# Odd token tiles carried to a later pair: layer two of a fused attention and MLP kernel, with another order of loads and an earlier first visit

## The chip, the cores and the metric

The kernel runs on one core of a Trainium2 chip. The metric is the device time of one execution in microseconds (us); less is better. TensorE is PE in the profile, VectorE DVE, ScalarE ACT, GpSimd POOL, SyncE SP.

## The reference

```python
def _attn_ref(q, k, v):                       # q, k, v: (8, 12, 448, 64), float32
    scores = q @ k.T / sqrt(64) - log(448)    # per batch and head
    attn = 1 / (1 + exp(-scores))             # sigmoid, no softmax
    return attn @ v
def _moe_ref(x, w_in, w_out, beta):           # x: (3584, 768); d_ff = 2048
    h = x @ w_in
    g = h * (1 / (1 + exp(-beta * h)))        # beta: one number per column of h
    return g @ w_out                          # (3584, 768), float32
# x is the attention output, heads side by side: 8 batches x 448 tokens, 12 x 64 columns
```

## The kernel before

Everything is computed in fp16 with fp32 sums in PSUM; the loads cast on the way. The 24 groups of four heads of a batch are called quads, three to a batch (QPB = 3).

**Attention in visits.** A visit computes the scores of one quad against 128 keys (jt = 0, 1, 2), or of one or two quads against the last 64 keys (jt = 3), into four PSUM banks, and one sigmoid on ACT (`weigh_two`, L257; `weigh`, L242 where it fills two banks) writes the weights to slots of the tile `attns`, which has 14 of them (NAT). From quad 3 on the visits stand in the list `visits`, numbered 0 to 73. `attend` (L332) multiplies a finished quad's weights with v; DVE copies the result to xT. The first batch goes in half visits, written out by hand in `BEGIN`.

**Layer one.** The first two batches are done by plain matmuls (`dense1`, L354), in groups of six, each followed by a sigmoid on ACT (L366) and a product on DVE (L369) that writes the hidden tile `gt`. Batches 2 to 7 go in pairs through `blocks`: a scheme of seven products for two batches at once (L523), 168 matmuls with 16 others between them. `first_layer` runs such a block at the visit that `turns` names. `gt` holds two batches (896 tokens, a window of NTILE = 7 tiles of 128), so each window is overwritten by the next.

**Layer two.** The 28 tiles of tokens are multiplied with w_out in halves of 384 columns. A pair of neighbouring tiles t and t + 1 goes by `strassen` (L643): seven products of eight matmuls, 56 in all. The sums of hidden halves that the products read are made on DVE two products ahead (`hidden_sum`, L630). A plain tile (`dense2`, L384) takes 32. Since a window has seven tiles, one is odd: in window 0 tiles 0, 1, 2 are plain and 3 to 6 two pairs; in windows 1 to 3 there are three pairs and a single tile (13, 20, 27) by `single` (L437), of 32 matmuls. The last tile's products are cut in pieces of 256 and 128 columns (CUTS), which ACT copies out (L399) and `store` writes.

**What sets the order.** The matmuls of layers one (plain) and two stand in a list `fill`. After each visit the loop at the end spends some of them: a pace, so that what is left spreads over the visits up to the next turn, plus a correction per visit from the table MORE (in units of 0.164 us); LATE says after how many matmuls attention values may go. TensorE's order is thus fixed when the kernel is built. `hidden_sum`, copies and transposes go to DVE's queue, loads to POOL's queue in the order of the lists LOADS and LATER and then of the visits, at most eight in flight; stores go to SP's queue.

Of the kernel before, what the change touches and what calls it, by code (L numbers as in the profile page):

```python
# [13 lines left out]
def kernel(  # L14
# [84 lines left out]
    NAT = 14  # L99
# [275 lines left out]
    def release(key):  # L375
        touch(held.pop(key))
        m2s.pop(key)
# [16 lines left out]
    def leave(t: int, half: int, m2, piece=None):  # L394
        lo, hi = half * HALF, (half + 1) * HALF
        if piece is not None:
            release((t, half, piece))
            lo, hi = CUTS[piece : piece + 2]
            nc.scalar.copy(out=osbs[t][:, lo:hi], in_=m2)  # L399
            store(t, lo, hi)  # L400
            return
# [5 lines left out]
        if t == NT - 1:  # L407
            store(t, lo, hi)
        elif left[t] == 2:
            store(t, 0, DM)  # L410

    CUTS = (0, 2 * P, HALF)

    def sum_of_halves(t: int):
        sums[t, 0] = sump.tile([P, ND, P], FP16, tag="sum", name="sum")
        nc.vector.tensor_tensor(out=sums[t, 0], in0=hid(t, 0), in1=hid(t, 1), op=ALU.add)

    def single(t: int, n: int, dc: int, piece=None):

        if (n, dc) == (0, 0):  # L420
            if (t, 0) not in sums:
                sum_of_halves(t)
            for half in range(1 + (t < NT - 1)):
                m2s[t, 1 - half] = bank(HALF, (t, 1 - half))
        if piece is not None and (n, dc) == (1, 0):
            m2s[t, 0, piece] = bank(CUTS[piece + 1] - CUTS[piece], (t, 0, piece))
        both = sums[t, 0]
        half, x, w = (
            (1, hid(t, 0), B12),
            (0, hid(t, 1), B21),  # L430
            (1, both, B22),
            (0, both, B11),
        )[n]
        m2 = m2s[(t, half) if piece is None else (t, half, piece)]
        stop = n > 1 and dc == ND - 1
        w = w[:, dc] if piece is None else w[:, dc, CUTS[piece] : CUTS[piece + 1]]
        nc.tensor.matmul(m2, x[:, dc], w, start=(n < 2 and dc == 0), stop=stop)  # L437
        if stop:
            leave(t, half, m2, piece)

    NT = NTOK // P

    def cols(t: int):
        return slice(t % NTILE * P, (t % NTILE + 1) * P)

# [186 lines left out]
    def strassen(t: int, i: int, dc: int):  # L632

        name, x, _, op, w = product(t, i)
        if dc == (ND // 2 if i == 0 and t % NTILE == 0 else 0) and i + 2 < NPROD:
            hidden_sum(t, i + 2)
        if (t, i, dc) == (NT - 3, NPROD - 2, 0):
            sum_of_halves(NT - 1)
        first = (t, name) not in m2s
        if first:  # L640
            m2s[t, name] = bank(HALF, (t, name))
        m2 = m2s[t, name]
        nc.tensor.matmul(  # L643
            m2,
            (x if op is None else sums[t, i])[:, dc],
            w[:, dc],
            start=first,
            stop=(dc == ND - 1),
            skip_group_check=i >= 4,
        )  # L650
        if dc < ND - 1:
            return
        if i == 0:
            for u in (t, t + 1):
                osbs[u] = outp.tile([P, DM], FP32, tag="osb", name="osb")
        L, R = slice(0, HALF), slice(HALF, DM)
        o1, o2 = osbs[t], osbs[t + 1]
        r, a = m2s.get((t, "r")), m2s.get((t, "a"))

        def add(out, in0, in1, op=ALU.add):  # L660
            nc.vector.tensor_tensor(out=out, in0=in0, in1=in1, op=op)  # L661

        if i == 1:
            nc.scalar.copy(out=o2[:, L], in_=a)  # L664
        elif i == 2:
            nc.vector.tensor_copy(out=o1[:, L], in_=m2)
            add(o1[:, R], r, o1[:, L])
            release((t, "s"))
        elif i == 3:
            add(o2[:, L], m2, o2[:, L])  # L670
            release((t, "b"))
        elif i == 4:
            add(o2[:, R], a, o2[:, L], ALU.subtract)
# [11 lines left out]
    def store(t: int, lo: int, hi: int):  # L685
        osb = osbs[t]
        c, end = t * P, (t + 1) * P
        while c < end:
            b, i = divmod(c, S)
            rows = out[b * S : (b + 1) * S, lo:hi]  # L690
            if b == B - 1:
                n = min(end - c, S - i, P if t == NT - 1 else ROWS)
# [9 lines left out]
    def pairs(first: int, n: int):  # L702
        for t in range(first, first + 2 * n, 2):
            for i in range(NPROD):
                for dc in range(ND):
                    opens = i in (2, 3) or (i == 4 and dc < ND // 2)
                    yield M2_US, lambda a=(t, i, dc): strassen(*a), opens

    def alone(t: int):
        order = [(n, None) for n in range(4)]  # L710
        if t == NT - 1:
            order = [(0, None), (2, None), (1, 0), (3, 0), (1, 1), (3, 1)]
        for n, piece in order:
            for dc in range(ND):
                yield M2_US, lambda a=(t, n, dc, piece): single(*a), n < 3
# [27 lines left out]
    def window(w: int):  # L743
        yield from pairs(w * NTILE, 3)
        yield from alone((w + 1) * NTILE - 1)
# [11 lines left out]
    with tc.manual_schedule():  # L757
        def load(what, *a):
# [21 lines left out]
            ("qk", 3), ("w_out", 0, 0), ("w_out", 1, 0), ("values", 1), ("qk", 4), ("qk", 5), ("w_out", 0, 1),  # L780
# [24 lines left out]
        still = const.tile([P, 512], FP16, name="still")  # L805
# [16 lines left out]
        def beta_columns():  # L822
# [14 lines left out]
            ("q", 3, 0), ("q", 3, 1), ("dense", 45),  # L837
# [29 lines left out]
        fill += list(pairs(3, 2))  # L867
# [17 lines left out]
        def left_us(n: int):  # L885
# [4 lines left out]
        MORE = {  # L890
# [3 lines left out]
        }  # L894
        RESERVE = (1.99, 3.28)
        LATE = {
            0: 1, 6: 1, 8: 3, 17: 1, 26: 6, 34: 4, 45: 2, 48: 3, 68: 10, 72: 10,
        }
        turns = {4 * QPB: 1, 6 * QPB: 1}
# [35 lines left out]
        def first_layer(b: int):  # L935
# [5 lines left out]
            fill.extend(window(b // 2))  # L941
            blocks(b, fill_units, 2 if b < B - 2 else 0)

        for n, (g, jt, also) in enumerate(visits):
# [17 lines left out]
            some_sum()  # L962
            for f in soon[:2]:
                f()
# [8 lines left out]
            owed = pace + MORE.get(n, 0) * M2_US  # L973
# [3 lines left out]
            while due or (at_fill[0] < len(fill) and fill[at_fill[0]][0] / 2 < owed):  # L977
                if due and (jt >= 1 or clear()) and spent >= LATE.get(n, 0):
                    values(due.pop())
                elif fill[at_fill[0]][0] / 2 < owed or (due and spent < LATE.get(n, 0)):  # L980
# [4 lines left out]
        assert not sums_todo  # L985
        due.append(NQUAD - 1)
# [32 lines left out]
```

## Time and profile before

| | |
|---|---|
| median of 3 runs | 373.27 us (373.2 to 373.52) |
| profiled execution | span 371.2 us from the first to the last instruction; what lies around it is the 2.1 us up to the median |
| granted TensorE clock | 0.999 |
| TensorE matmul | 365.5 us busy, 98% |
| DVE / ACT / POOL | 254.4 / 259.7 / 80.5 us busy |
| first visit of the list, first matmul | 42.12 us |
| last visit (73), first matmul | 298.07 us |
| last matmul, start | 367.77 us |

A line of a timeline is: start, duration, engine, line, operation, what it writes <- what it reads, shape, number, and in brackets the engine's idle time before it with what ended it. A line of waits is: who waited, for whom, us in total, how often, the longest.

### The profile page before, as it was taken

The page shows a single profiled execution, that of the slowest core. Times are in us where ns is not written, and L with a number is a line of the kernel's source. Part 1 is how long each engine was busy: PE and PEld are TensorE (multiplying, and loading weights), DVE is VectorE, ACT ScalarE, POOL GpSimd, SP SyncE. Part 2 cuts the span into 40 slices and gives each one's busy share as a digit, 9 for nine tenths or more (in the row PEclk, how much of TensorE's full clock was granted, in tenths as well). Part 3 has the DMA queues.
Part 4 walks back from the last instruction along what each step waited for, and adds up shares of the span by engine and source line. Part 5 has one row for each costly group of instructions (what it writes and reads, how often), then busy time and mean ns, then how long its engine had stood idle before and what let it go on. Part 6 is the DMA issues. An engine that isn't in the chain of part 4 may idle for free.

```text
span 371.2 us, 7295 instructions
## 1 busy us (share of the span) xinstructions
PE 365.5 (98%) x2906; PEld 184.6 (50%) x2906; DVE 254.4 (69%) x479; ACT 259.7 (70%) x311; POOL 80.5 (22%) x120
## 2 busy tenths in 40 slices
PE   8999999999999999999999999999999999999997
PEld 4566544443444455544444445554444455555665
DVE  4435796777496967787666667778767667679671
ACT  5995766798967668887877749887678647883000
POOL 7732431221131013233131003233100002230000
PEclk9999999999999999999999999999999999999999
DMA  9999999893368030029829410017803111000334
GB/s 173 195 197 204 202 205 206 193 123 51 51 86 174 1 87 1 2 49 130 171 37 212 106 25 20 3 29 110 171 2 85 44 44 42 1 2 1 87 85 129
DMA packets 36226, 34.65 MB, mean 93 GB/s; under 512 B 9424, under 2 KB 32608, under 8 KB 36192
## 3 DMA queue, kind: packets, MB, share of 16 engines
q0 software_dynamic: 30288, 22.47, 42.3%
q1 hardware_dynamic: 5904, 11.71, 11.1%
q8 instruction: 23, 0.38, 0.4%
q14 instruction: 11, 0.09, 0.1%
HBM read 45.62 MB, written 11.01 MB: 153 GB/s over the span
## 4 chain that ended last, share of the span: by engine, by line
PE 93%; ACT 5%; issue 1%; DVE 0%; ACTq 0%
PE ps L643 27%; PE ps L523 26%; PE ps L229 11%; PE ps L332 10%; PE ps L354 9%; PE ps L384 4%; PE ps L437 4%; ACT attns L242 3%; ACT attns L257 1%; PE ps L812 1%; ACT sg L366 1%; DVE gt L369 0%; ACT osb L664 0%; DVE still L806 0%; ACT osb L399 0%
## 5 line engine op out<-in xcount | busy, mean ns | idle before, releaser
L257 ACT ACTIVATE attns<-ps,nlogs 128x1792 f16<-128x1792 f32 x75 | 131.7, 1756 | 41.1 <-PE ps L229 41.0
L643 PEld LDWEIGHTS <-sum 128*128 128x128 f16 x440 | 40.5, 98 | 37.3 <-issue 12.5
L537 POOL TENSOR_TENSOR gt<-attns,sg 128x448 f16<-128x448 f32 x21 | 23.9, 1137 | 141.7 <-ACT sg L534 141.7
L229 PE MATMUL ps<-qT,kT 32*128 32x448 f16 (+3 forms) x864 | 52.3, 339 | 1.1 <-ACT attns L242 0.6
L534 ACT ACTIVATE sg<-ps,beta_sb 128x448 f32<-128x448 f32 x72 | 45.2, 632 | 8.4 <-PE ps L523 5.9
L523 PE MATMUL ps<-xT,w_in 128*128 128x448 f16 x216 | 49.2, 353 | 0.0
L523 PE MATMUL ps<-xT,w_S 128*128 128x448 f16 x216 | 49.2, 352 | 0.0
L643 PE MATMUL ps<-w_T,sum 128*128 128x384 f16 x264 | 48.7, 327 | 0.0
L537 DVE TENSOR_TENSOR gt<-ps,sg 128x448 f16<-128x448 f32 x72 | 44.2, 618 | 4.0 <-ACT sg L534 3.8
L341 DVE CAST xT<-ps 128x448 f16<-128x448 f32 (+1 forms) x54 | 28.8, 567 | 21.5 <-PE ps L332 21.5
L523 PEld LDWEIGHTS <-w_in 128*128 128x128 f16 x288 | 28.0, 98 | 26.6 <-issue 0.7
L661 DVE TENSOR_TENSOR osb<-ps,osb 128x384 f32<-128x384 f32 x55 | 30.5, 554 | 15.1 <-PE ps L643 12.8
L332 PE MATMUL ps<-attns,v 128*64 128x448 f16 (+3 forms) x432 | 40.4, 340 | 0.1
L354 PE MATMUL ps<-xT,w_in 128*128 128x448 f16 (+1 forms) x240 | 39.5, 316 | 0.6 <-DVE gt L369 0.6
L630 DVE TENSOR_TENSOR sum<-gt 128x1024 f16<-128x1024 f16 x55 | 36.5, 678 | 0.2
L369 DVE TENSOR_TENSOR gt<-ps,sg 128x448 f16<-128x448 f32 (+1 forms) x40 | 20.0, 527 | 22.4 <-ACT sg L366 22.3
L125 POOL DMA_DIRECT2D raw<-in_q_dram x26 | 14.4, 555 | 92.8 <-DVE kT L212 84.7
L643 PE MATMUL ps<-w_out,gt 128*128 128x384 f16 x176 | 33.3, 327 | 0.0
L643 PE MATMUL ps<-w_out,sum 128*128 128x384 f16 x176 | 32.3, 327 | 0.0
L583 DVE TENSOR_TENSOR ps<-ps,attns 128x448 f32<-128x448 f32 x24 | 15.2, 632 | 23.3 <-PE ps L523 19.4
L523 PEld LDWEIGHTS <-w_S 128*128 128x128 f16 x216 | 21.1, 98 | 19.4
L354 PEld LDWEIGHTS <-w_in 128*128 128x128 f16 x240 | 22.0, 98 | 16.9 <-issue 5.8
(52 smaller groups left out, 364.3 us busy)
## 6 DMA issues: line engine op xcount, KB each, us to landing
out_dram<-osb SPq DMA_DIRECT2D x100, 96.0 KB, 2.2
raw<-in_k_dram POOLq DMA_DIRECT2D x23, 224.0 KB, 5.3
raw<-in_q_dram POOLq DMA_DIRECT2D x21, 224.0 KB, 4.1
v<-in_v_dram POOLq DMA_DIRECT2D x16, 192.0 KB, 6.9
w_in<-in_moe_w_in_dram POOLq DMA_DIRECT2D x8, 384.0 KB, 11.9
w_out<-in_moe_w_out_dram POOLq DMA_DIRECT2D x4, 768.0 KB, 15.0
v<-in_v_dram POOLq DMA_DIRECT2D x16, 144.0 KB, 7.5
out_dram<-osb SPq DMA_DIRECT2D x5, 144.0 KB, 2.4
```

Of the source, the lines that this page charges most:

```text
L229: nc.tensor.matmul(sco[base : base + nk, hh, u0 : u0 + n], kT[g][lo : lo + BLK, jt * P : jt * P + nk, e], qT[g][lo : lo + BLK, c0 : c0 + n ...
L257: nc.scalar.activation(out=attns[:, slot : slot + 2].rearrange("p n h s -> p (n h) s"), in_=sco, func=AF.Sigmoid, bias=nlogs[:, 0:1], scal ...
L332: nc.tensor.matmul(av[hh * D : (hh + 1) * D, 0:n], vs[b][base : base + nk, 2 * (s % NPAIR) + hh, jt], at[base : base + nk, hh, 0:n], start ...
L341: nc.vector.tensor_copy(out=xTs[b][:, s % NPAIR, c0 : c0 + n], in_=av[:, 0:n])
L354: nc.tensor.matmul(m1, w_in16[:, hc, dc * P : (dc + 1) * P], xTs[b][:, hc, c0 : c0 + n], start=(hc == 0), stop=(hc == NHC - 1),)
L369: nc.vector.tensor_tensor(out=gt[:, dc, off : off + n], in0=m1, in1=sg[:, 0:n], op=ALU.mult)
L523: nc.tensor.matmul(out, w[:, c, i * P : (i + 1) * P], m[:, c], start=(start and c == 0), stop=(c == KH - 1), skip_group_check=not start,)
L534: nc.scalar.activation(out=sg, in_=h, func=AF.Sigmoid, bias=0.0, scale=beta_sb[:, dc : dc + 1])
L537: return lambda: engine.tensor_tensor(out=gt[:, dc, b % 2 * S : b % 2 * S + S], in0=h, in1=sg, op=ALU.mult)
L630: nc.vector.tensor_tensor(out=sums[t, i], in0=x, in1=y, op=op)
L643: nc.tensor.matmul(m2, (x if op is None else sums[t, i])[:, dc], w[:, dc], start=first, stop=(dc == ND - 1), skip_group_check=i >= 4,)
L661: nc.vector.tensor_tensor(out=out, in0=in0, in1=in1, op=op)
```

## The change

- `single` and the single tiles go. Tile 2 is kept and paired with tile 13 in window 1, tile 20 with tile 27 in window 3: `keep` copies a tile's hidden values on GpSimd from `gt` to a new tile `carry`, in four parts. `below(t)` names the partner. Window 0 has two plain tiles, window 1 four pairs, window 2 three, window 3 four.
- The cut in pieces moves from the last single tile to the a-products of the last pair, tiles 25 and 26; the results leave through the DVE additions of the pair.
- `attns` has 12 slots for 14; the constant tile of the warm-up matmuls lies in `gt`.
- In `LATER` the second quarter of w_out goes behind quads 4 and 5 and the v of batch 1.
- Ten dense matmuls instead of 45 stand at the end of `BEGIN`: 97 instead of 132 ahead of visit 0.
- The table MORE goes; LATE keeps one entry; the turns are at one and two visits later; the last eight matmuls of `fill` are held back from quad 6 on.

```diff
-    NAT = 14
+    NAT = 12
...
+    LAST = NT - 3
     CUTS = (0, 2 * P, HALF)
+    carry = const.tile([P, NDC, P], FP16, name="carry")
+    partner = {2: 2 * NTILE - 1, 3 * NTILE - 1: NT - 1}
...
+    def below(t: int):
+        return partner.get(t, t + 1)
+
+    def keep(t: int):
+        for r in range(4):
+            rows = slice(r * NDC // 4, (r + 1) * NDC // 4)
+            nc.gpsimd.tensor_copy(out=carry[:, rows], in_=gt[:, rows, cols(t)])
...
     def hid(t: int, half: int):
+        if t in partner:
+            return carry[:, half * ND : (half + 1) * ND]
         return gt[:, half * ND : (half + 1) * ND, cols(t)]
...
-        A11, A12, A21, A22 = hid(t, 0), hid(t, 1), hid(t + 1, 0), hid(t + 1, 1)
+        A11, A12, A21, A22 = hid(t, 0), hid(t, 1), hid(below(t), 0), hid(below(t), 1)
...
-    def strassen(t: int, i: int, dc: int):
+    def strassen(t: int, i: int, dc: int, piece=None):
...
+        lo, hi = (0, HALF) if piece is None else CUTS[piece : piece + 2]
+        key = (t, name) if piece is None else (t, name, piece)
...
         elif i == 5:
-            add(o2[:, R], r, o2[:, R])
-            release((t, "r"))
-            store(t + 1, 0, DM)
+            add(o2[:, R], m2, o2[:, R])
+            release(key)
+            store(below(t), 0, DM)
         elif i == 6:
-            add(o1[:, L], a, o1[:, L], ALU.subtract)
-            release((t, "a"))
-            store(t, 0, DM)
+            add(o1[:, L], m2, o1[:, L], ALU.subtract)
+            release(key)
+            store(t, lo, hi if t == LAST else DM)
...
-        yield from plain(((0, 0), (1, 0), (2, 0), (0, 1), (1, 1), (2, 1)))
+        yield from plain(((0, 0), (1, 0), (0, 1), (1, 1)))
...
-    def window(w: int):
-        yield from pairs(w * NTILE, 3)
-        yield from alone((w + 1) * NTILE - 1)
+    window = {
+        1: (7, 9, 11, 2),
+        2: (14, 16, 18),
+        3: (21, 23, 20, 25),
+    }
...
-            ("qk", 3), ("w_out", 0, 0), ("w_out", 1, 0), ("values", 1), ("qk", 4), ("qk", 5), ("w_out", 0, 1),
+            ("qk", 3), ("w_out", 0, 0), ("qk", 4), ("values", 1), ("qk", 5), ("w_out", 1, 0), ("w_out", 0, 1),
             ("w_out", 1, 1),
...
-        still = const.tile([P, 512], FP16, name="still")
+        still = gt[:, NDC - 1, 0:512]
...
-            ("q", 3, 0), ("q", 3, 1), ("dense", 45),
+            ("q", 3, 0), ("q", 3, 1), ("dense", 10),
...
-        MORE = {
...
-        LATE = {
-            0: 1, 6: 1, 8: 3, 17: 1, 26: 6, 34: 4, 45: 2, 48: 3, 68: 10, 72: 10,
-        }
-        turns = {4 * QPB: 1, 6 * QPB: 1}
+        LATE = {8: 3}
+        turns = {4 * QPB: 2, 6 * QPB: 3}
...
+            if b == 4:
+                keep(3 * NTILE - 1)
...
+            if n == 5:
+                keep(2)
...
-            owed = pace + MORE.get(n, 0) * M2_US
+            owed = pace
...
+            end = len(fill) - (ND if g >= 2 * QPB else 0)
...
+        fill_units(len(fill) - at_fill[0] - ND)
         due.append(NQUAD - 1)
```

More of the change, by code (lines that the diff above doesn't have):

```diff
@@ L392, in dense2, with leave @@
             leave(t, half, m2)
-    def leave(t: int, half: int, m2, piece=None):
+    def leave(t: int, half: int, m2):
         lo, hi = half * HALF, (half + 1) * HALF
[L396 to L401, printed above, removed]
         release((t, half))
@@ L406, in leave @@
         left[t] = left.get(t, 0) + 1
-        if t == NT - 1:
-            store(t, lo, hi)
-        elif left[t] == 2:
+        if left[t] == 2:
             store(t, 0, DM)
+    NT = NTOK // P
+    LAST = NT - 3
     CUTS = (0, 2 * P, HALF)
[L414 to L441, printed above, removed]
+    carry = const.tile([P, NDC, P], FP16, name="carry")
+    partner = {2: 2 * NTILE - 1, 3 * NTILE - 1: NT - 1}
     def cols(t: int):
         return slice(t % NTILE * P, (t % NTILE + 1) * P)
+    def below(t: int):
[4 more added lines that the diff above has]
+            nc.gpsimd.tensor_copy(out=carry[:, rows], in_=gt[:, rows, cols(t)])
     ND = NDC // 2
@@ L630, in hidden_sum @@
             nc.vector.tensor_tensor(out=sums[t, i], in0=x, in1=y, op=op)
-    def strassen(t: int, i: int, dc: int):
+    def strassen(t: int, i: int, dc: int, piece=None):
         name, x, _, op, w = product(t, i)
-        if dc == (ND // 2 if i == 0 and t % NTILE == 0 else 0) and i + 2 < NPROD:
+        if dc == (ND // 2 if i == 0 and t % NTILE == 0 else 0) and i + 2 < NPROD and not piece:
             hidden_sum(t, i + 2)
-        if (t, i, dc) == (NT - 3, NPROD - 2, 0):
-            sum_of_halves(NT - 1)
-        first = (t, name) not in m2s
+        lo, hi = (0, HALF) if piece is None else CUTS[piece : piece + 2]
+        key = (t, name) if piece is None else (t, name, piece)
+        first = key not in m2s
         if first:
-            m2s[t, name] = bank(HALF, (t, name))
-        m2 = m2s[t, name]
+            m2s[key] = bank(hi - lo, key)
+        m2 = m2s[key]
         nc.tensor.matmul(
@@ L645, in strassen @@
             (x if op is None else sums[t, i])[:, dc],
-            w[:, dc],
+            w[:, dc, lo:hi],
             start=first,
@@ L652, in strassen @@
             return
-        if i == 0:
-            for u in (t, t + 1):
+        if (t, 0) not in osbs:
+            osbs[t, 0] = None
+            for u in (t, below(t)):
                 osbs[u] = outp.tile([P, DM], FP32, tag="osb", name="osb")
-        L, R = slice(0, HALF), slice(HALF, DM)
-        o1, o2 = osbs[t], osbs[t + 1]
-        r, a = m2s.get((t, "r")), m2s.get((t, "a"))
+        L, R = slice(lo, hi), slice(HALF + lo, HALF + hi)
+        o1, o2 = osbs[t], osbs[below(t)]
+        r = m2s.get((t, "r"))
         def add(out, in0, in1, op=ALU.add):
@@ L663, in strassen @@
         if i == 1:
-            nc.scalar.copy(out=o2[:, L], in_=a)
+            nc.scalar.copy(out=o2[:, L], in_=m2)
         elif i == 2:
@@ L691, in store @@
             if b == B - 1:
-                n = min(end - c, S - i, P if t == NT - 1 else ROWS)
+                n = min(end - c, S - i, P if t == LAST else ROWS)
                 to = rows[i : i + n]
@@ L700, with pair, pairs @@
     M1_US, M2_US = 0.148, 0.164
-    def pairs(first: int, n: int):
-        for t in range(first, first + 2 * n, 2):
-            for i in range(NPROD):
+    def pair(t: int):
+        for i in range(NPROD):
+            opens = i in (2, 3)
+            for piece in (0, 1) if t == LAST and product(t, i)[0] == "a" else (None,):
                 for dc in range(ND):
[L706 to L715, printed above, removed]
+                    us = M2_US if piece is None else (0.11, 0.056)[piece]
+                    yield us, lambda a=(t, i, dc, piece): strassen(*a), opens or (i == 4 and dc < ND // 2)
+    def pairs(*tiles):
+        for t in tiles:
+            yield from pair(t)
     def plain(tiles):
@@ L866 @@
         L1E = len(fill)
-        fill += list(pairs(3, 2))
+        fill += list(pairs(3, 5))
         sums_todo = [(in_sum, n, p, 0) for n in ("S3", "S2", "S4") for p in range(2)]
@@ L940, in first_layer @@
             fill_units(len(fill) - at_fill[0] - ND)
-            fill.extend(window(b // 2))
+            fill.extend(pairs(*window[b // 2]))
             blocks(b, fill_units, 2 if b < B - 2 else 0)
+            if b == 4:
+                keep(3 * NTILE - 1)
         for n, (g, jt, also) in enumerate(visits):
@@ L976 @@
             spent = 0
-            while due or (at_fill[0] < len(fill) and fill[at_fill[0]][0] / 2 < owed):
+            end = len(fill) - (ND if g >= 2 * QPB else 0)
+            while due or (at_fill[0] < end and fill[at_fill[0]][0] / 2 < owed):
                 if due and (jt >= 1 or clear()) and spent >= LATE.get(n, 0):
                     values(due.pop())
-                elif fill[at_fill[0]][0] / 2 < owed or (due and spent < LATE.get(n, 0)):
+                elif at_fill[0] < end and (fill[at_fill[0]][0] / 2 < owed or (due and spent < LATE.get(n, 0))):
                     spend()
```

9 lines of the change are left out of this document (5 added, 4 removed), and 3 rows, old and new, of the table MORE.

## The prediction

> **What bounds the kernel now.** I read the page first (span, busy shares, DMA slices), then the waits of TensorE, the chain of waits, and the timeline of three stretches. In the page the second line is the busy share of each engine, the third the DMA share in 40 slices of 9.28 us.
>
> ```profile
> span 371.2 us, 7295 instructions
> PE 365.5 (98%) x2906; PEld 184.6 (50%) x2906; DVE 254.4 (69%) x479; ACT 259.7 (70%) x311; POOL 80.5 (22%) x120
> DMA  9999999893368030029829410017803111000334
> ```
> TensorE is the bound, and the DMA engines are full for the first 74 us: in that stretch what lands when depends on the order of issue. All of TensorE's waits:
>
> ```profile
> PE ps L812 <- DVE still L806: 1.2, 1, 1.2
> PE ps L229 <- ACT attns L242: 0.6, 2, 0.4
> PE ps L354 <- DVE gt L369: 0.6, 1, 0.6
> ```
> So a matmul less is time less, unless a wait appears. How near the waits are shows the timeline of three visits (start, duration; PE, then ACT):
>
> ```profile
> 175.75 0.58 PE L229 MATMUL ps<-qT,kT 32*128 32x448 f16 x8
> 176.26 1.96 PE L643 MATMUL ps<-w_out,gt 128*128 128x384 f16 x11
> 178.18 0.58 PE L229 MATMUL ps<-qT,kT 32*128 32x448 f16 x8
> 178.69 1.64 PE L332 MATMUL ps<-attns,v 64*64 64x448 f16 x16
> 180.26 0.50 PE L643 MATMUL ps<-w_out,gt 128*128 128x384 f16 x2
> 180.70 0.57 PE L229 MATMUL ps<-qT,kT 32*128 32x448 f16 x8
> ...
> 176.38 1.75 ACT L257 ACTIVATE attns<-ps,nlogs 128x1792 f16<-128x1792 f32 x1 [0.45 <-PE ps L229]
> 178.81 1.75 ACT L257 ACTIVATE attns<-ps,nlogs 128x1792 f16<-128x1792 f32 x1 [0.68 <-PE ps L229]
> ```
> A visit's scores fill four PSUM banks, the sigmoid (L257) empties them, and only then may the next scores start. Scores to sigmoid 176.38 - 175.75 = 0.63, sigmoid 1.75, its end to the next scores 178.18 - 178.13 = 0.05: no visit takes less than 2.43 us. TensorE needs 0.51 for the scores, 0.164 for a 384-column matmul and about 0.09 for the change of kind: 2.40 with eleven matmuls between, so a visit of eleven already sits on the floor. A visit of twelve takes 2.56; with attention values (16 matmuls, 1.57) and two more, 180.70 - 178.18 = 2.52. The kernel before never gives a visit with that sigmoid less than this.
>
> **The change, part by part.** Visits carry the kernel's own numbers, 0 to 73; visit 0 starts at 42.12. What each holds in the changed kernel I counted in the built order of its matmuls.
>
> *Products.* Tiles 2 and 13, 20 and 27 become two pairs: 13 pairs of 56 and two plain tiles of 32 make 792 matmuls of 384 columns, against 808 (eleven pairs, three plain, three single tiles). The last pair's a-products are cut in 256 and 128 columns; eight of each take 0.87 + 0.44 = 1.31 at the end of the trace (365.58, 366.45, 367.33, 367.77), as eight whole ones do. So 16 x 0.164 = 2.6 us of TensorE work go. They go unevenly: up to the start of visit 4 24 fewer, visits 4 to 72 14 fewer, from visit 73 on 22 more.
>
> *Start.* 35 dense matmuls (23 of 448 columns at 0.187, 12 of 224 at 0.099: 84 took 12.57, twelve of 224 1.2) move behind visit 0. TensorE is ready for visit 0 at 42.12 - 5.5 = 36.6. But its scores read these two:
>
> ```profile
> 36.59 0.69 DVE L212 STREAM_TRANSPOSE kT<-raw 128x256 f32<-128x256 f32 x2
> 37.21 0.66 DVE L200 STREAM_TRANSPOSE qT<-raw 128x224 f32<-128x224 f32 x2
> ```
> They keep their place in DVE's queue behind gates that wait for the 39 matmuls before them. So visit 0 starts at 37.87 + 0.05 = 37.9, a wait of 1.3. Visit 0 (eleven dense of 448, one of 224) takes 2.78, visits 1 and 2 (6 of 448, 11 of 224) 2.83 each. Visit 3 starts at 46.35 and holds one dense and ten plain matmuls. The ninth plain one reads rows 8 to 15 of w_out, wanted at 46.35 + 0.52 + 0.10 + 0.09 + 8 x 0.164 = 48.4. This load now stands behind quads 4 and 5 (four of 224 KB) and batch 1's v (672 KB). Before, it released its slot at 41.35, by the POOL line at 41.64, whose issue waited for it:
>
> ```profile
> 41.64 0.53 POOL L125 DMA_DIRECT2D raw<-in_k_dram  x1 [3.15 <-DMA w_out<-in_moe_w_out_dram]
> ```
> 1568 KB at the 202 GB/s of the 42 to 69 us window are 7.95 us: 49.3. (The trace's own landing of the last of the same set is 49.35.) TensorE waits another 1.0, and visit 4 starts at 49.4 + 2 x 0.164 + 0.09 = 49.8; before, 51.31: **-1.5**. Bounds: were the load in time, 48.8 (-2.5); if it is 1 us later, -0.5. I take the landing, since the order fixes the bytes ahead of it.
>
> *Visits 4 to 72.* Fourteen matmuls fewer: -2.3. But a visit with fewer meets the floor. Visits that need less than 2.43 (2.47 where both halves of keys 384 to 447 are scored): before, 18 of eleven matmuls at 0.03 to 0.05 and three of values plus one at 0.1, together 0.84. After: twelve of ten at 0.19 to 0.21, one of nine at 0.35, four of values plus one at 0.1, 13 of eleven at 0.03 to 0.05: 3.48. The two blocks of fused first-layer products keep their content; the same tariff gives 246.6 for the trace's 246.8 of the kernel before. The pacing tables (MORE, LATE, turns) act through these counts alone. **-2.3 + 2.64 = +0.3**, bounds -0.5 and +1.
>
> *Visit 73 to the last matmul* has no floor, 22 more matmuls: **+3.6**.
>
> *Tail.* Before, the last three stores leave 366.37, 367.93 and 368.71, the last 0.33 after the last matmul ends (368.38), and land 1.5 later. Now three stores of tile 26 (48, 48, 32 rows) are released by the add after product r, which ends 1.31 before the last matmul; that add takes 0.56 and SP issues one store per 0.44 (362.47 to 364.69). From the end of r: stores at 0.7, 1.1, 1.55, the 256-column piece 2.0, the last 2.45 instead of about 1.6. **+0.8**, bounds 0.3 and 1.2. The add on DVE in place of ACT's copy costs nothing either way: ACT's 128x128 took 0.27, DVE's 128x224 cast 0.35.
>
> *Carried tiles.* Twice four copies of 128x512 on POOL. No row has such a copy; POOL's product of 128x448 takes 1.137, DVE's rows of this size 0.3 to 0.7: 0.3 to 1.3 each, up to 5.2 for four. Queued behind them are the loads of quad 7 and v of batch 2 (issued from 51.24 before, now from 55 at worst, landing 60 to 65 behind a full DMA queue, wanted from 67) and the loads of quad 21 (wanted 8 us later, landing in 4 to 5). I take 0; without that cover up to 1.5. Beside them DVE runs sums that read two SBUF tensors (L630, 678 ns). In the trace POOL's L537 and DVE's sums hardly meet, so the row is no proof. By the Trainium skill (SBUF — State Buffer, "Who interferes with whom") a DVE operation with two SBUF inputs and a GpSimd one that reads SBUF block each other for a whole instruction. By that rule the sums stand still while the copies run, and the time would be that of the last rival below; by the rows alone the sum stays.
>
> *Smaller edits.* Twelve slots for fourteen: a slot's reader is TensorE, and scores stand behind it in TensorE's own order, so no wait; later first layers only give their sums more time; the memset in gt is as long as the one in still. Nothing each; a slot that were late would hold a sigmoid for one set of attention matmuls at most, 1.6 once. DVE's weight sum of visit 6 waits for the last quarter of w_out, here from about 55 to 57.0; behind it stand a copy out of a PSUM bank, with two more banks free, and transposes wanted at 59: nothing, and 2 without that cover.
>
> **Sum.** -1.5 + 0.3 + 3.6 + 0.8 = +3.2 on the span of 371.2: 374.4. The median of the runs shown, 373.27 (373.2 to 373.52), is 2.1 above the span; I keep that: 376.4.
>
> **Rivals.** *Work alone counts* (the other side): the floor and both early waits don't hold since TensorE always has something ready, as its 98% say; -2.6 with the tail's 0.8 gives 371.5. It decides where a visit of ten matmuls takes 2.26 and not 2.43. Against it stand 21 visits pinned at 2.43 to 2.48, TensorE's strict order and the ninth plain matmul's wait. 6%. *Floor half real* (scores of a visit begin on the first two banks while ACT still reads the others): the floor's 2.64 shrinks to nearly nothing, 373.8. One ACT instruction covers all four banks, so against. 7%. *w_out in time*: only the transposes' 1.3 is waited for, 375.4. The bytes ahead say no. 12%. *Copies in the way*: four copies of up to 1.14 hold DVE's sums for 4.6; a sum is asked for two products (16 matmuls and a visit's scores, some 3.6) ahead, so the product waits 1.0, twice, with the loads behind the copies: 377.4 to 378.4. 10%. That the change doesn't make the products it names is excluded by the count. Forecast 65%.
>
> **How the numbers follow.** Likeliest 376.4, its own range 375.5 to 377.3. A measurement of this kernel tells about 0.2% (0.75 us) from no change. The range 374.6 to 377.8 adds the w_out case and half of the copies, and leaves out the two low rivals and the copies' upper half. Faster 0.06 (work alone), slower 0.87, same 0.07 (floor half real).
>
> **What would show it.** Visit 0's scores near 37.9 behind L200; a wait of the ninth plain matmul for a DMA near 49.3; visits of ten matmuls at 2.43; visit 73 near 296.7 (298.07 before); the last matmul near 370.9 and the last store over 1 us behind it. Wrong: visits of ten at 2.26, visit 4 before 48.9, or TensorE waiting for DVE's sums.

## The result and the profile after

The changed kernel takes **378.66 us** (median of four, 378.54 to 379.15) against 373.33 (373.2 to 373.52) for the kernel before: 1.0144 times as long, interval 1.013 to 1.0157. The forecast was 376.4, range 374.6 to 377.8: the direction was right, and the size was 2.3 us too small, outside the range. The profiled execution took 378.54 with a span of 376.6, so the span grew by 5.4 where the sum had 3.2.

The head of the page (span, busy time by engine, DMA share in 40 slices):

```profile
span 376.6 us, 7314 instructions
PE 365.2 (97%) x2898; PEld 185.2 (49%) x2898; DVE 261.6 (69%) x493; ACT 259.7 (69%) x312; POOL 86.6 (23%) x128
DMA  9999999863295030078459311003913030002332
```
TensorE has eight instructions fewer than before and is busy 0.3 less, in a span 5.4 longer, so it is idle for 5.7 more. By count 16 x 0.164 = 2.6 us of its work went, so part of what is booked as busy is likely to be waiting. DVE has 7.2 us more busy time and POOL 6.1 (eight copies of the carried tiles among it).

All of TensorE's waits (line waited for, us in total, times, longest):

```profile
PE ps L229 <- ACT attns L257: 1.5, 7, 0.3
PE ps L229 <- DVE qT L200: 1.2, 1, 1.2
PE ps L791 <- DVE gt L785: 1.2, 1, 1.2
PE ps L229 <- ACT attns L242: 0.6, 2, 0.4
PE ps L384 <- DMA w_out<-in_moe_w_out_dram: 0.6, 1, 0.6
PE ps L229 <- DVE kT L212: 0.5, 1, 0.5
PE ps L354 <- DVE gt L369: 0.5, 1, 0.5
```
Rows one, two, five and six are new. The first is the floor of the visits (scores that wait for the sigmoid), and it shows only 1.5 of it: where a wait is short or the group before it runs late, nothing is booked. So the visits' starts have to be compared too.

| place | before | after | added |
|---|---|---|---|
| visit 0 starts | 42.12 | 37.94 | |
| visit 4 starts | 51.31 | 50.00 | -1.3 |
| visits 4 to 72 | 246.76 | 248.79 | +2.0 |
| visit 73 to the last matmul's start | 70.09 | 73.69 | +3.6 |
| from there to the end of the span | 3.0 | 4.1 | +1.1 |

The sum is +5.4. The last matmul here is the very last one, which starts at 368.16 before and at 372.48 after; the 367.77 of the table of the kernel before is the start of the last eight.

*The start,* from the timeline (start, duration, engine, line, work; in brackets the idle time before it and what ended it):

```profile
37.22 0.66 DVE L200 STREAM_TRANSPOSE qT<-raw 128x224 f32<-128x224 f32 x2
37.94 0.57 PE L229 MATMUL ps<-qT,kT 32*128 32x448 f16 x8 [1.24 <-DVE qT L200]
...
49.00 0.48 PE L384 MATMUL ps<-w_out,gt 128*128 128x384 f16 x2 [0.58 <-DMA w_out<-in_moe_w_out_dram]
49.28 0.66 DVE L212 STREAM_TRANSPOSE kT<-raw 128x256 f32<-128x256 f32 x2
50.00 0.57 PE L229 MATMUL ps<-qT,kT 32*128 32x448 f16 x8 [0.52 <-DVE kT L212]
```
Three waits in series: visit 0 for its transposes, the ninth plain matmul for w_out, and behind it visit 4 for the transposes of its keys, which stand on DVE behind a weight sum, a copy and another transpose.

*A visit of the new kind.* Visit 54 holds six product matmuls and the 16 of attention values. Its scores start at 215.31:

```profile
216.07 0.69 DVE L212 STREAM_TRANSPOSE kT<-raw 128x256 f32<-128x256 f32 x2
216.15 0.81 PE L620 MATMUL ps<-w_T,sum 128*128 128x384 f16 x4
216.69 0.52 DVE L639 TENSOR_TENSOR osb<-ps,osb 128x384 f32<-128x384 f32 x1
216.89 0.11 PEld L332 LDWEIGHTS <-v 64*64 64x64 f16 x3 [0.32 <-issue]
216.89 2.00 PE L332 MATMUL ps<-attns,v 64*64 64x448 f16 x16
217.27 0.10 PEld L332 LDWEIGHTS <-v 64*64 64x64 f16 x1 [0.27 <-issue]
217.57 0.90 PEld L332 LDWEIGHTS <-v 128*64 128x64 f16 x12 [0.20 <-issue]
```
The row of the 16 matmuls takes 2.00 us here, where the same row without a wait takes 1.64 (178.69 in the prediction's timeline; its 1.57 is the time up to the next group's start). Three weights go in, then a gap: the fourth is loaded at 217.27, just after DVE's addition (L639) has ended at 217.21. That addition empties a PSUM bank of the product just finished, and it stands on DVE behind a transpose of 0.69. No line of the waits names it, since TensorE is counted as busy throughout. The visit takes 3.52 where its work needs 3.16.

*The tail,* from the timeline:

```profile
371.42 0.56 DVE L639 TENSOR_TENSOR osb<-ps,osb 128x384 f32<-128x384 f32 x1 [0.58 <-PE ps L620]
372.29 0.74 DVE L639 TENSOR_TENSOR osb<-ps,osb 128x256 f32<-128x256 f32 x2 [0.32 <-PE ps L620]
```
The addition after product r ends at 371.98 and releases three stores of tile 26; with the two of the last piece, five are issued between 372.04 and 373.86, and the last lands at 375.70.

### The profile page after: what moved, and what is told of

Its sections match the earlier page's. It is cut to its first block, busy times and chain, and to the rows that moved or that the text cites. A ratio compares the mean times of both kernels' runs of the same rounds, so it can differ in the third digit from the quotient of the medians.

```text
span 376.6 us, 7314 instructions
## 1 busy us (share of the span) xinstructions
PE 365.2 (97%) x2898; PEld 185.2 (49%) x2898; DVE 261.6 (69%) x493; ACT 259.7 (69%) x312; POOL 86.6 (23%) x128
## 4 chain that ended last, share of the span: by engine, by line
PE 82%; ACT 12%; DVE 2%; issue 2%; DMA 1%; ACTq 0%; DVEq 0%
PE ps L620 28%; PE ps L498 25%; PE ps L229 11%; PE ps L332 10%; ACT attns L257 7%; PE ps L354 7%; ACT attns L242 3%; ACT sg L366 1%; DMA gt<-in_k_dram 1%; PE ps L384 1%; DVE gt L369 1%; DVE w_S L458 0%; DVE kT L212 0%; DVE qT L200 0%; DVE osb L639 0%
## 5 line engine op out<-in xcount | busy, mean ns | idle before, releaser
L620 PEld LDWEIGHTS <-sum 128*128 128x128 f16 x536 | 49.0, 98 | 42.2 <-issue 13.0
L620 PE MATMUL ps<-w_T,sum 128*128 128x384 f16 (+2 forms) x328 | 57.4, 319 | 0.0
L639 DVE TENSOR_TENSOR osb<-ps,osb 128x384 f32<-128x384 f32 (+2 forms) x67 | 36.1, 540 | 13.9 <-PE ps L620 12.9
L332 PE MATMUL ps<-attns,v 128*64 128x448 f16 (+3 forms) x432 | 42.0, 340 | 0.1
L498 PEld LDWEIGHTS <-w_in 128*128 128x128 f16 x288 | 28.1, 98 | 26.4 <-issue 0.4
L620 PE MATMUL ps<-w_out,sum 128*128 128x384 f16 x208 | 38.2, 327 | 0.0
L607 DVE TENSOR_TENSOR sum<-gt 128x1024 f16<-128x1024 f16 x57 | 38.0, 688 | 0.2
L620 PE MATMUL ps<-w_out,gt 128*128 128x384 f16 (+2 forms) x200 | 36.3, 320 | 0.0
L369 DVE TENSOR_TENSOR gt<-ps,sg 128x448 f16<-128x448 f32 (+1 forms) x40 | 20.1, 527 | 22.9 <-ACT sg L366 22.6
L229 PEld LDWEIGHTS <-kT 32*128 32x128 f16 (+1 forms) x864 | 15.8, 96 | 32.8 <-issue 28.0
```

The lines of the kernel that those rows point to most:

```text
L229: nc.tensor.matmul(sco[base : base + nk, hh, u0 : u0 + n], kT[g][lo : lo + BLK, jt * P : jt * P + nk, e], qT[g][lo : lo + BLK, c0 : c0 + n ...
L332: nc.tensor.matmul(av[hh * D : (hh + 1) * D, 0:n], vs[b][base : base + nk, 2 * (s % NPAIR) + hh, jt], at[base : base + nk, hh, 0:n], start ...
L369: nc.vector.tensor_tensor(out=gt[:, dc, off : off + n], in0=m1, in1=sg[:, 0:n], op=ALU.mult)
L498: nc.tensor.matmul(out, w[:, c, i * P : (i + 1) * P], m[:, c], start=(start and c == 0), stop=(c == KH - 1), skip_group_check=not start,)
L607: nc.vector.tensor_tensor(out=sums[t, i], in0=x, in1=y, op=op)
L620: nc.tensor.matmul(m2, (x if op is None else sums[t, i])[:, dc], w[:, dc, lo:hi], start=first, stop=(dc == ND - 1), skip_group_check=i >= 4,)
```

## Experiments

My theory after the result had four parts: the start's waits are in series, so that one removed exposes the next; the floor is real, so that matmuls taken out of visits of eleven bring nothing; the 1.7 us that the sum lacked in visits 4 to 72 come mostly from banks that the values wait for; and the tail is a queue of stores. Rivals: that the missing time lies in contention (POOL's copies, DVE's busier queue), or that the floor is only half real.

**1. The transposes earlier** (e1_transposes).

```diff
-            ("dense", 39), ("k", 3), ("q", 3, 0), ("q", 3, 1), ("dense", 10),
+            ("dense", 28), ("k", 3), ("q", 3, 0), ("q", 3, 1), ("dense", 21),
```


> Changed kernel, but the transposes of quad 3 are queued after 28 dense matmuls instead of 39 (97 ahead of visit 0 as before). Theory (two waits in series: whatever is gained at visit 0 is waited for again at the ninth plain matmul, whose load lands at 49.0): visit 0 at 36.7 instead of 37.94, that wait grows from 0.6 to about 1.8, visit 4 at 49.4 to 50.0 instead of 50.00, time 378.0 to 378.7 against 378.66. Rival (the transposes alone cost the start): visit 4 at 48.8, time 377.4.

Measured 379.83 (378.38 to 379.99), ratio 1.017 (1.0151 to 1.0189). In the profiled execution visit 0 starts at 36.76, 1.2 earlier, and visit 4 at 49.98. The wait moved on:

```profile
PE ps L384 <- DMA w_out<-in_moe_w_out_dram: 2.3, 1, 2.3
```
So the early transposes alone gained nothing here. Part of that is this execution's loads: they came some 0.55 later from the first quarter of w_out on (37.63 against 37.09), and the wait ended at 49.57. Had it ended at 49.00 as in the changed kernel, visit 4 would have come 0.6 earlier, half of the 1.2. The expectation left that open (49.4 to 50.0). The median is above that of the changed kernel by 1.2 because three of the four executions had a mean granted clock of 0.995 and took 379.8 to 380.0; the profiled one had 1.000 and took 378.38.

**2. The second half of w_out in its old place** (e2_w_out).

```diff
-            ("qk", 3), ("w_out", 0, 0), ("qk", 4), ("values", 1), ("qk", 5), ("w_out", 1, 0), ("w_out", 0, 1),
+            ("qk", 3), ("w_out", 0, 0), ("w_out", 1, 0), ("values", 1), ("qk", 4), ("qk", 5), ("w_out", 0, 1),
```


> Changed kernel, but the second quarter of w_out is loaded in its old place, ahead of the v of batch 1 and of quads 4 and 5. Theory (behind the wait for the load stands another: DVE's transposes of quad 4, which end at 49.94 whatever w_out does): the wait of 0.6 goes, visit 4 starts at 49.9 to 50.0 as now, time 378.5 to 378.7. Rival (the load is what delays visit 4): visit 4 at 49.0 to 49.4, time 377.7 to 378.1.

378.69 (378.48 to 378.82), ratio 1.0147 (1.0132 to 1.0163): no gain either. Visit 4 stands 12.06 behind visit 0, as in the changed kernel. (In 4, 5, 6, 7 and 9, which share that start, visit 0 lies between 37.91 and 38.57 and visit 4 always 12.06 or 12.07 behind it.) It waits for

```profile
PE ps L229 <- DVE kT L212: 1.4, 2, 1.3
```
The rival "w_out in time" of the prediction, 375.4, falls with this: w_out was in time, and the next wait had the same end.

**3. Both** (e3_both, the two edits above together).

> Both edits together. Theory: each alone gives little, both together take away the first two waits and leave DVE's transposes of quad 4, 1.2 earlier: visit 4 at 48.8, time 377.4 against 378.66. Rival (the effects add): the sum of what the two runs before gave.

377.65 (377.11 to 379.08), ratio 1.0126 (1.0105 to 1.0147): the median is 1.0 below the changed kernel's, where the expectation was 377.4. The one execution with a mean clock of 1.000 took 377.11, 1.4 less than the changed kernel's fastest, 378.54. The profiled execution is the slowest, 379.08, and visit 4 starts at 49.47 in it, not at 48.8, after a wait of 1.7 for the kT transposes. Part of this wait has a cause of its own. A weight sum that stands ahead of the transposes on DVE, first in the changed kernel and then here, where it starts 0.03 after a copy of the carried tile on POOL:

```profile
47.35 0.95 DVE L458 TENSOR_TENSOR w_S<-w_in,w_S 128x1536 f16<-128x1536 f16 x1
```
```profile
46.31 0.63 POOL L419 COPY carry<-gt 128x512 f16<-128x512 f16 x1
46.34 1.43 DVE L458 TENSOR_TENSOR w_S<-w_in,w_S 128x1536 f16<-128x1536 f16 x1
```
The sum takes 0.48 longer. Visit 4 stands 12.55 behind visit 0 here, 0.48 more than the 12.07 above; without the copy it would have come near 49.0.

The windows of this execution (busy time and count for PE, PEld, DVE, ACT, POOL; then granted clock, DMA share, GB/s):

```profile
47.00:50.00 3.00, 1.26 (x17) 0.36 (x15) 2.94 (x7) 0.30 (x1) 0.25 (x1) 1.00 1.25 203
50.00:51.00 1.00, 1.00 (x14) 0.51 (x12) 1.00 (x2) 0.90 (x1) 1.00 (x2) 0.85 1.31 204
51.00:54.00 3.00, 3.00 (x19) 0.83 (x16) 2.38 (x6) 1.12 (x2) 3.00 (x6) 0.50 1.31 203
54.00:55.00 1.00, 1.00 (x8) 0.56 (x7) 0.63 (x2) 1.00 (x1) 1.00 (x2) 0.94 1.32 207
```
TensorE was busy 1.26 of the three us before 50, and from 50.7 on it ran at half its clock for some 3.4 us. Visits 4 to 72 take 250.03 here against 248.79. So a long wait costs its own length, and in this execution 1.2 us more.

**4. One transpose behind the fill at three visits** (e4_bank): at visits 25, 54 and 58 the transpose that DVE had ahead of the addition is issued after the visit's matmuls.

```diff
-            if jt in (0, 1) and QPB < g < NQUAD - 1:
+            if jt in (0, 1) and QPB < g < NQUAD - 1 and n not in (25, 54, 58):
                 transpose(g + 1, jt)
...
+            if n in (25, 54, 58):
+                transpose(g + 1, jt)
```


> Changed kernel, but at visits 25, 54 and 58 the transpose of the next quad's q or k goes to DVE's queue behind the visit's fill instead of ahead of it. TensorE's order is the same. Theory (attention values there take the PSUM bank of the product that has just ended, and its eviction on DVE stands behind a transpose of 0.64 to 0.70): the three visits take 3.33, 3.16 and 3.16 instead of 3.63, 3.52 and 3.52, time down by 0.7 to 1.0 to 377.7 to 378.0. Rival (the 0.3 are a cost of going over from products to values in the middle of a visit): the visits stay at 3.5 to 3.6 and the time at 378.6.

377.74 (377.72 to 377.8), ratio 1.0123 (1.0106 to 1.014): 0.9 less, as expected. In the profiles, visits 4 to 72 take 248.12 against 248.79, 0.7 less. The same place as above, visit 54:

```profile
216.21 0.56 DVE L639 TENSOR_TENSOR osb<-ps,osb 128x384 f32<-128x384 f32 x1 [0.25 <-issue]
216.70 0.23 PEld L332 LDWEIGHTS <-v 64*64 64x64 f16 x4 [0.32 <-issue]
216.70 1.76 PE L332 MATMUL ps<-attns,v 64*64 64x448 f16 x16
217.13 0.90 PEld L332 LDWEIGHTS <-v 128*64 128x64 f16 x12 [0.20 <-issue]
```
The addition starts as soon as the product is done and ends at 216.77; four weights go in without a gap, and the 16 matmuls take 1.76. Visits 25, 54 and 58 take 3.45, 3.28 and 3.28 (3.63, 3.52, 3.52 before the edit). The work alone, which the expectation had named, would be 3.33, 3.16, 3.16: two thirds of the wait is gone (0.66 us, which is the whole difference of the profiles), and the addition's own 0.56 still covers the start of the values. So the bank wait is shown at these three visits, and the queue ahead of the addition is most of it.

**5. The last stores thinned** (e5_tail): tile 26's left half leaves after product b; its right half as one store of 128 rows.

```diff
+            if t == LAST:
+                store(below(t), 0, HALF)
...
-            store(below(t), 0, DM)
+            store(below(t), HALF if t == LAST else 0, DM)
...
-                n = min(end - c, S - i, P if t == LAST else ROWS)
+                n = min(end - c, S - i, P if t in (LAST, LAST + 1) else ROWS)
```


> Changed kernel, but of the last pair's lower tile (26) the left half is stored as soon as it is done, after the product b, and the right half as one store of 128 rows, so that one store instead of three stands on SP's queue ahead of the two last pieces. Theory (the tail grew by 1.1 because three stores of 0.37 to 0.5 each were queued ahead of the last ones): the span ends 0.6 to 1.0 earlier, 377.6 to 378.1. Rival (the landing of the last piece or the add on DVE sets the end): 378.5 to 378.8.

378.21 (377.79 to 378.63), ratio 1.0122 (1.0102 to 1.0142): above the expected range. Three executions took 377.8 to 378.0 and three 378.4 to 378.6, so the time doesn't settle it. Visit 0 started 0.44 later in this profile, so the tail is measured from visit 73: to the last landing 75.99, against 76.90. Three stores go at 372.45, 373.19 and 373.62 in place of five, and the last lands 1.6 behind its start. So 0.9 of the tail was the queue of stores.

**6. More work in the visits of ten** (e6_pad): nine visits of ten (26, 27, 28, 31, 62, 64, 66, 69, 71) get an eleventh matmul of 384 columns, with zeros as its operand, so that it adds nothing to the product.

```diff
+    def more_work(m2, x):
+        while padded[0]:
+            padded[0] -= 1
+            nc.tensor.matmul(m2, x, zeros, start=False, stop=False, skip_group_check=True)
...
+            padded[0] = {26: 1, 27: 1, 28: 1, 31: 1, 62: 1, 64: 1, 66: 1, 69: 1, 71: 1}.get(n, 0)
```


> Changed kernel with nine more matmuls of 384 columns, one in each of the visits 26, 27, 28, 31, 62, 64, 66, 69 and 71, which have ten; they add zeros to a product. 9 x 0.164 = 1.48 us of TensorE work. Theory (these visits sit on the floor of 2.43 to 2.49 that scores, sigmoid and their hand-overs set): the visits stay as long as they are, time 378.6 to 378.9. Rival (TensorE's work counts): the visits grow by 0.16 each, time 380.0 to 380.2.

The time, 379.1 (378.52 to 381.23), ratio 1.016 (1.0131 to 1.0188), is too spread to settle it, and visit 0 started 0.6 later in the profile. The visits do: 4 to 72 take 248.78, against 248.79 without the nine. Visit 26 in the changed kernel and then in this one:

```profile
109.37 0.57 PE L229 MATMUL ps<-qT,kT 32*128 32x448 f16 x8
109.88 1.80 PE L620 MATMUL ps<-w_T,sum 128*128 128x384 f16 x10
110.05 1.75 ACT L257 ACTIVATE attns<-ps,nlogs 128x1792 f16<-128x1792 f32 x1 [1.95 <-PE ps L229]
111.86 0.57 PE L229 MATMUL ps<-qT,kT 32*128 32x448 f16 x8 [0.18 <-ACT attns L257]
```
```profile
110.00 0.58 PE L229 MATMUL ps<-qT,kT 32*128 32x448 f16 x8
110.51 0.34 PE L629 MATMUL ps<-w_T,sum 128*128 128x384 f16 x1
110.68 0.33 PE L616 MATMUL ps<-zeros,sum 128*128 128x384 f16 x1
110.68 1.75 ACT L257 ACTIVATE attns<-ps,nlogs 128x1792 f16<-128x1792 f32 x1 [1.95 <-PE ps L229]
110.84 1.63 PE L629 MATMUL ps<-w_T,sum 128*128 128x384 f16 x9
112.49 0.58 PE L229 MATMUL ps<-qT,kT 32*128 32x448 f16 x8
```
Both are 2.49 from scores to scores. 9 x 0.164 = 1.48 us of TensorE work cost nothing: the floor is whole, not half. It is also 2.49 and not 2.43 here, since the sigmoid starts 0.68 after the scores, where most start after 0.62. What delays it no run tested.

**7. One pair instead of two** (e7_one_pair): only tiles 2 and 13 are paired; 20 and 27 are single tiles, and the tail is that of the kernel before.

```diff
-    partner = {2: 2 * NTILE - 1, 3 * NTILE - 1: NT - 1}
+    partner = {2: 2 * NTILE - 1}
...
-    LAST = NT - 3
+    LAST = NT - 1
```


> Changed kernel, but only tiles 2 and 13 are paired; tiles 20 and 27 are single as in the kernel before, and the last tile ends as there (ACT copies of the pieces). Eight matmuls more in all: 32 more up to visit 73, 24 fewer behind it. Theory: work +1.3, floor of the visits 55 to 72 gone (-1.4), one wait for a PSUM bank less (-0.35), tail as before (-1.1): 376.9 to 377.3. Rival (work counts): 380.0 with the tail as it is, 378.9 with the old one.

377.27 (377.12 to 377.58), ratio 1.0099 (1.008 to 1.0118): eight matmuls more than the changed kernel, 1.3 us of work, and 1.4 us less. In the profiles: the start +0.3, visits 4 to 72 +2.9 (visits of 13 at 2.73, none on the floor late in the kernel), visit 73 to the last matmul -3.4, the tail -1.1. The second pair moved work from in front of visit 73 to behind it, paid the floor in front and the stores at the end.

**8. A version built from these** (e8_combined): one pair and the old tail, as in 7; twelve dense matmuls fewer ahead of visit 0; the transposes of quads 3 and 4 earlier on DVE, those of quad 5 a visit later, and the w_out quarter before quad 5; DVE's sums later; both first-layer blocks a visit earlier; the plain tiles' right halves in two parts; a third matmul beside the values at visits 15 and 18; and the late transpose of 4 at visits 30 and 53.

```diff
-            ("values", 2, 1), ("dense", 39), ("k", 3), ("q", 3, 0), ("q", 3, 1), ("dense", 10),
+            ("values", 2, 1), ("dense", 28), ("k", 3), ("q", 3, 0), ("q", 3, 1), ("dense", 9),
...
-            ("qk", 5), ("w_out", 1, 0), ("w_out", 0, 1),
+            ("w_out", 1, 0), ("qk", 5), ("w_out", 0, 1),
...
-        LATE = {8: 3}
+        LATE = {8: 3, 15: 3, 18: 3}
...
+            if g == QPB + 1 and jt in (1, 2):
+                transpose(g + 1, jt - 1)
...
+            if (g, jt) == (QPB, 2):
...
+            if late_t and jt in (0, 1) and QPB + 1 < g < NQUAD - 1:
+                transpose(g + 1, jt)
```


> What the theory would do: one pair (2, 13) as in the run before; visit 0 behind 85 dense matmuls with quad 3's transposes queued after 28 of them; quad 4's transposes a visit earlier and quad 5's a visit later; the second quarter of w_out ahead of quad 5; weight sums only from visit 9 on; the two right halves of the plain tiles in two parts by rows; first layers at one and two visits after quads 12 and 18; transposes behind the fill at visits 30 and 53. 800 matmuls, floor 1.05 us by the tariff that gave 0.84 for before. Expected: visit 0 at 35.4, no wait over 0.6 after it, 372.0 to 372.8, against 373.2 of the kernel before. If waits of DVE or of loads come in their place, 373.5 to 375.

**372.95** (372.79 to 373.34, twelve executions) against 373.55 for the kernel before in the same batch of runs, ratio 0.9983 (0.9972 to 0.9994). The expectation was 372.0 to 372.8, so it is 0.15 above that range. The page and TensorE's waits:

```profile
span 371.0 us, 7297 instructions
...
PE ps L844 <- DVE gt L838: 1.2, 1, 1.2
PE ps L229 <- ACT attns L242: 0.6, 2, 0.4
PE ps L229 <- ACT attns L257: 0.5, 2, 0.3
PE ps L354 <- DVE gt L369: 0.5, 1, 0.5
PE ps L660 <- DVE osb L679: 0.4, 1, 0.4
```
The three waits of the start are gone together: visit 4 starts at 46.95, 3.3 earlier than in 7, and that is most of the 4.3 between the two (visits 4 to 72 give 0.7 and the stretch behind visit 73 gives 0.2). It is below the kernel before by less than 0.2%. The interval just excludes no change, but the kernel before ranged from 372.98 to 374.08 in the same batch (and once 375.58), and the two profiled spans are 371.0 and 371.2: I count it as a tie.

**9. Three matmuls beside the values at visits 15 and 18** (e9_values_later), where two had been, on the changed kernel.

```diff
-        LATE = {8: 3}
+        LATE = {8: 3, 15: 3, 18: 3}
```


> Changed kernel, but at visits 15 and 18 the attention values go after three dense matmuls of the visit and not ahead of them. Theory (as at visits 25, 54 and 58, the values want a PSUM bank whose gate on ACT and DVE isn't done): visits 15 and 18 take 2.75 with three dense matmuls, where they took 2.81 and 2.79 with two: 0.44 less for the same work, time 378.2 of 378.66. Rival (those visits are long for another reason): 2.99 each, time unchanged.

378.43 (378.31 to 378.98), ratio 1.0137 (1.0123 to 1.0151); visits 15 and 18 take 2.75 and 2.83, about as long with three dense matmuls as with two (2.81, 2.79): a third one is free or nearly so. At visit 15 that is the expected 2.75, which its work needs; visit 18 is 0.08 longer. Visits 4 to 72 are 0.4 shorter, since visit 25 now has five product matmuls beside the values instead of seven and takes 3.30 instead of 3.63. The median's 0.2 is no more than the spread; the visits carry this one.

**10. The version of 8 with both pairs** and the tail of 5 (e10_two_pairs). The edit is shown against 8.

```diff
-    partner = {2: 2 * NTILE - 1}
+    partner = {2: 2 * NTILE - 1, 3 * NTILE - 1: NT - 1}
...
-        turns = {4 * QPB: 1, 6 * QPB: 2}
+        turns = {4 * QPB: 1, 6 * QPB: 3}
...
-            late_t = n in (30, 53)
+            late_t = n in (30, 54, 58)
```


> The combined version with both pairs (2 and 13, 20 and 27), that is eight matmuls fewer than with one, and the tail of the run e5; transposes behind the fill at visits 30, 54 and 58, first layers at one and three visits after quads 12 and 18. Theory (the second pair takes its matmuls out of visits that then sit on the floor and adds 24 behind the last visit): work 1.3 less, floor 1.7 more than in the combined version, 373.2 to 373.9. Rival (eight matmuls fewer are worth 1.3 once the waits are gone): 371.6 to 371.9.

373.86 (373.62 to 374.15, eleven executions), ratio 1.0012 (1.0003 to 1.0021). As expected; eight matmuls fewer than in 8 and 0.9 slower, with the transposes behind the fill and the stores thinned: visit 73 starts 2.9 earlier, the stretch behind it is 3.6 longer, the tail 0.3. The second pair does not pay in this order of work.

## Why the prediction was wrong by 2.3

- **Visit 0, -1.5 at visit 4.** Forecast 37.9, measured 37.94, behind L200 as named. The wait of the ninth plain matmul came as named, at 49.00 instead of 49.3. What I did not see was the third wait, of visit 4's scores for DVE: 50.00 and not 49.8. The term is -1.3. That it is off by only 0.2 is partly luck: the load came 0.3 earlier than forecast, and the unseen wait added 0.5. Experiments 1 to 3 show that it is a series: either edit alone brought nothing (the first at most 0.6, had the load come as before), and both brought 1.0 by the medians, 1.4 by the fastest executions.
- **Visits 4 to 72, +0.3, bounds -0.5 and +1: the step that failed.** They took 248.79, 2.0 more than before where the term had 0.3, so 1.7 is missing in it. (By the forecast's terms visit 73 starts at 296.9 and the last matmul at 370.6; the 296.7 and 370.9 that it names do not follow from them.) The floor, which was the bulk of the term, held: visits of ten took 2.43 to 2.54, the two visits with the fused first-layer products 36.99 each, which is what the matmuls in them took before, and experiment 6 shows that the floor is complete. What failed is the sentence that the pacing tables act through the counts alone: in the changed kernel's order the attention values of three visits stand behind six or seven product matmuls, right at the end of a product, and a wait for a PSUM bank was put at nothing. Five visits (25, 54, 58 and 15, 18) have values that follow a product or gate whose bank DVE is still emptying: 0.30, 0.36, 0.36, 0.25 and 0.23 above their work, 1.5 together. Experiment 4 took 0.7 of the three's 1.0 back by moving three transposes. For the other two, 9 shows that something other than work sets their length; that it is the bank is read from the trace alone (in visit 15 the first of two gates on DVE, L369, ends at 79.36, and the values' third matmul starts at 79.41). I counted matmuls for each visit, and not which bank the next group takes or what stands ahead of its eviction on DVE, though the text had looked at DVE's queue for the start. The remaining 0.2 may be the sigmoid at 0.68 in eight visits on the floor (8 x 0.06 = 0.5, two of which lay on it before too), read from the trace and not tested by a run.
- **Visit 73 to the last matmul, +3.6.** Measured 73.69 against 70.09: +3.6. Experiment 7 gave 3.4 of it back with one pair fewer.
- **Tail, +0.8, bounds 0.3 and 1.2.** The mechanism was as told; it measured +1.1. Product r ends near 371.4, and the five stores leave 0.65, 1.0, 1.5, 2.0 and 2.5 behind it, as forecast (0.7 to 2.45). What was mis-sized is the landing: 375.70 - 373.86 = 1.8 for the last store with four close ahead of it, where I kept the 1.5 of before. Experiment 5, with three stores in place of five, took 0.9 off the tail.
- **Carried tiles, 0.** The eight copies took 0.61 to 1.34 on POOL, and no wait names them. The rival "copies in the way" is not what made the time longer, although 378.4 lay near. But the hold that it rests on is in the trace. Two of DVE's hidden sums (L607) that start during a copy, at 256.28 and 258.14, took 0.80 and 1.09, where all others took 0.65 to 0.69; the copy that the second one met had itself taken 0.95, begun during another sum. By the Trainium skill (SBUF — State Buffer, "Who interferes with whom") sums that meet the copies stand still while a copy runs, and the trace agrees: each of the two ends 0.54 after its copy. In the changed kernel that is 0.5 us of DVE's time at visits 56 and 57, which stayed on the floor (2.48 and 2.43), so it cost nothing; in experiment 3 a sum held in this way stood ahead of TensorE's wait. The rival was wrong in how often they meet, not in the mechanism.
- **Rivals.** "Work alone counts" and "floor half real" are excluded by the visits of ten (none below 2.43) and by experiment 6; "w_out in time" by experiment 2.
- **Smaller edits, nothing each:** no wait of the trace names one, and no run tested them alone.

So: -1.3 + 2.0 + 3.6 + 1.1 = +5.4, against -1.5 + 0.3 + 3.6 + 0.8 = +3.2. Of the 2.2 missed, 1.7 lie in visits 4 to 72, 0.3 in the tail and 0.2 in the start. The direction came true; the range was too narrow because the bound of +1 for the visits stood on no mechanism, such as the bank.

## What to carry to other kernels

Where another engine's loop sets the length of each step, removing matmuls from steps that are already on that floor gains nothing, and moving the rest behind the last step costs in full: count the work step by step, whatever the busy share says. Beside the count, look for each step at which PSUM bank its next group takes, which instruction empties it, and what stands ahead of that on its engine; such a wait can hide inside a group that the profile counts as busy. Waits at the start of a kernel often stand in series, so test them together as well as one at a time.

## What the hardware showed that I had not expected

TensorE's wait of 1.7 us in experiment 3 was followed by granted clocks of 0.85, 0.50 and 0.94 in the windows of one, three and one us from 50 on. The loss is 0.15 + 3 x 0.50 + 0.06 = 1.7 us of clock; at half clock that is 3.4 us of such time. Visits 4 to 72 grew by 1.2 for it. Experiment 1, with its wait of 2.3, had a mean clock of 0.995 in three of four executions and took about 1.5 longer in these; the changed kernel, whose longest wait is 1.2, had 1.000 in all four. So a wait can cost more than half its own length again. That the wait brings the half clock is seen in one trace only, and it need not be the only cause: one of 17 executions of the kernel before, whose longest wait in its trace is 1.2, also had 0.995 (375.58 us). The Trainium skill (TensorE: Matmul & The Clock Gate, "What's actually happening") has the clock at half or full, decided by a free-running window of about 3.4 us. The length and the chance from execution to execution agree with these runs; the Trainium skill asks for an idle window, while here about 1.7 us of waiting, in three us with TensorE busy for 1.26, were enough.

The other one is the hold between GpSimd and VectorE above: it shows as a longer duration of the held instruction (1.43 for 0.95, 1.09 for 0.68), not as a wait.
